# Attention beside a token-mixing MLP on one core: the first bias loaded in rows and turned over on TensorE, and a table of scheduling numbers by stretch

## The chip, the cores and the metric

One core of a Trainium2 chip runs the whole kernel. Its engines are TensorE (PE; its weight loads are shown apart as PEld), VectorE (DVE), ScalarE (ACT), GpSimd (POOL) and SyncE (SP, which issues most DMAs). The metric is device time in microseconds for one execution; the median of several executions is compared. Durations of single instructions come from one profiled execution.

## The reference

The input `x` has 2048 rows (tokens) of 512 columns, in bf16. It is layer-normalised; the result feeds an attention of 32 heads of 16 columns and, normalised once more, an MLP that mixes tokens: its matrices run over the 2048 tokens and a hidden width of 1376.

```
def _A_ref(x, wqkv, wo):
    qkv = split of (x @ wqkv) into q, k, v of 32 heads, 16 wide
    p = softmax(q @ k^T * 16 ** -0.5)
    return (p @ v, heads joined) @ wo

def _B_ref(x, w1, b1, w2, b2):
    h = _layernorm(x)
    u = gelu(einsum("bsd,sf->bdf", h, w1) + b1)
    y = einsum("bdf,fs->bds", u, w2) + b2
    return y transposed back to (b, s, d)

xn = _layernorm(A_x)
return A_x + _A_ref(xn, A_wqkv, A_wo) + _B_ref(xn, B_w1, B_b1, B_w2, B_b2)
```

`b1` has 1376 values, one for each hidden unit: ten rows of 128 and one of 96.

## The kernel before, in words

**Attention.** Queries are taken in 4 stretches of 512, heads in 8 groups of four: 32 blocks, worked in order. A block has 16 tiles of 128 keys, so there are 512 *groups* (block, key tile). The scores of a group are four matmuls (one for each of four heads, 32 rows of the array each, `score_mm`, L615) into four PSUM banks of 128 keys by 512 queries. A group goes one of two ways:

- On ACT ("A"): two `exp_tile` instructions (L638), each over two banks, write bf16 into `pT`. One set of four matmuls (`pv_mm`, L651) then multiplies by V into the block's PSUM bank (bank 6).
- On DVE ("D"): the exponential is made by arithmetic on the bits of a bf16. `dve_first` (L698) turns one bank into 16-bit integers, four times a group ("first step"); that is a plane. Two more planes are the first one plus a constant, made whole by one DVE instruction (`add_plane`, L711) or one POOL instruction (`add_plane_pool`, L718). Each of the three planes is multiplied by V in a set of its own, so a D group needs three sets of L651 where an A group needs one. `dve_first2` does the first step of two neighbouring banks in one instruction; the table before never allows it (`PAIR` is 0).

ACT rotates over banks 0 to 3. D scores use banks 4, 5 and 7, and so do all other products (the "chains": projections of q, k, v, both MLP layers, the output projection).

**Other work, in chains.** A `Chain` is a list of steps on named engines with a due position and a release position, counted in blocks. `chain_ut` makes one of the 11 hidden tiles of the MLP: 16 matmuls, then a DVE instruction (`u_evac`, L976) that adds the bias column `b1h[:, ft]`. `gelus` runs the gelu on ACT (L987). `chain_yo` makes the output rows. `chain_epi` ends a block: DVE copies the sums out of bank 6 (L1212), DMAs carry the denominators to DRAM and back (`den_scr`, `den_s`, `rec_scr`, `denb`), and POOL multiplies (L1249). `chain_qt` brings the next q rows into `QT` with eight DMAs on SP.

In most chains a 128-row product is issued as four matmuls of 32 output rows (`mm`, L541 to L555; L548 is a matmul, L547 a transpose). Such a quad is called a *unit*: at 512 columns it takes about as long as one full matmul.

**Order.** All instructions are put into a static order for each engine when the program is built. A dispatcher (`Sched` and the loop in the kernel function) keeps a clock for each engine with a cost for each instruction (917 ns for an exponential, 226 ns for a 512-column unit, 95 ns for a change between scores and other products, 450 ns for the issue of a DMA). At each moment it chooses what the engine does next: `pe_step` for PE (which also decides which group goes to ACT and which to DVE), `dve_step` for DVE, `misc_step` for POOL and SP. These choices depend on sixteen numbers:

```
TOL, JOIN, DEFER, P1_PRI, D_PEND, FAR, D_HUNGRY, PACE, N_SAME, PRESS, PL_PRI, D_LAST, SEED, PAIR, POOL_MIN, BURST
```

For example, `JOIN` is how long PE may wait for a DVE bank so that D scores join A scores in one visit; `POOL_MIN` is how much backlog DVE must have before POOL takes a plane; `PAIR` allows `dve_first2`; `SEED` varies some limits pseudo-randomly. The table `POLICY` holds rows of these numbers. Row n is read when the dispatcher's clock passes n times `SEG` = 10,000 ns, and the last row stays in force. Before, it has one row, so it holds throughout. Where PE has less than a given weight of units in the last 3.4 us of the dispatcher's clock, `pe_step` adds a filler: a unit of zeros accumulated into bank 6.

**The bias before.** At the start DVE clears `b1c_bf` (L442, 128 x 11), and two DMAs on SP fill it from the flat vector (L366), one value per partition, each value a 2-byte piece. Later, in `late_consts` (run once the work is a little past the first block), POOL turns it into fp32 in `b1h` (L460). `late_consts` also issues the loads of `wo_c` and `wo_pad`, and the first loads of `w1` and `w2` follow it on SP.

Of the kernel before, what the change touches and what calls it, by code (L numbers as in the profile page):

```python
# [10 lines left out]
BF16 = mybir.dt.bfloat16  # L11
# [8 lines left out]
F = 1376  # L20
NT = S // 128
NCT = D // 128
NFT = (F + 127) // 128
# [70 lines left out]


SEG = 10000.0
POLICY = [(130.0, 150.0, 300.0, -1, 0, 1300.0, 0.0, 0.05, 2, 3, 2, 7500.0, 0, 0.0, 1000.0, 2)]


SWITCH = 95.0  # L100
# [174 lines left out]
def bass_parallel_sum__softmax_full_mha__mixer_token_mlp__prompt_kernel(  # L275
# [18 lines left out]
    with ExitStack() as es:  # L294
        block = es.enter_context(nc.Block())

        def sb(name, shape, dt):
            return es.enter_context(nc.sbuf_tensor(name, shape, dt))
# [27 lines left out]
        w1blk = w1_flat[:, :].rearrange("p (s t j) -> p s t j", s=NW1, j=128)  # L326
        plx = sb("plx", [128, 2 * 2048], BF16)
        w2blk = sb("w2blk", [128, NW2, NFT, 128], BF16)
        b1c_bf = sb("b1c_bf", [128, NFT], BF16)
        b1h = sb("b1h", [128, NFT], F32)  # L330
        ident = sb("ident", [128, 128], BF16)
        stats = sb("stats", [128, NT, 6], F32)
# [6 lines left out]
        zw = sb("zw", [128, 128], BF16)  # L339
# [9 lines left out]
        sc = Sched(nc, es)  # L349
# [4 lines left out]
        PV_BANK = 6  # L354
        EX_BANK = 7

        def T_DVE(n, div=1.0):
            return dict(occ=(n / div + 64.0) / 0.96, lat=(n / div + 64.0) / 0.96 + 141.0)
# [3 lines left out]
        def dma(q, dst, src, reads, writes, name="", noncontig=False, out_dma=False, lat=2500.0, move=150.0):  # L362
            if noncontig:
                def fn(eng, dst=dst, src=src):
                    with nc.allow_non_contiguous_dma(reason="small strided transfer"):
                        return eng.dma_start(dst, src)  # L366
            else:
                def fn(eng, dst=dst, src=src):
                    return eng.dma_start(dst, src)
            op = sc.add(q, fn, reads=reads, writes=writes, name=name, dma=True, out_dma=out_dma, occ=450.0, lat=lat)  # L370

            dma_free[0] = max(dma_free[0], op.start + 1300.0) + move
            op.end = max(op.end, dma_free[0] + 700.0)
            heapq.heappush(sc.marks, op.end)
            return op
# [9 lines left out]
               reads=[("ident",)], writes=[("ident",)], occ=270, lat=400)  # L385
# [18 lines left out]
        for r in range(4):  # L404
            sc.add("pool", lambda e, r=r: e.memset(qmask[32 * r:32 * r + 16, 0:1], QSCALE),
                   reads=[("qmask",)], writes=[("qmask",)], occ=135, lat=145)
        sc.add("pool", lambda e: e.tensor_scalar(qmask[:, 1:2], qmask[:, 0:1], -1.0, QSCALE, ALU.mult, ALU.add),
               reads=[("qmask",)], writes=[("qmask",)], occ=190, lat=260)
# [14 lines left out]
        for t in range(NPRE):  # L423
            dma("sp" if t < 2 else "act", x_sb[:, t, :], x2[128 * t:128 * t + 128, :],
                reads=[("ident",)] if t == 2 else [], writes=[("x", t)], name="ld_x", lat=2150 + 150 * t)
# [4 lines left out]
               occ=1500)  # L430
# [8 lines left out]
        NFTF = F // 128  # L439
        MLAST = F - 128 * NFTF  # L440

        sc.add("dve", lambda e: e.memset(b1c_bf[:], 0.0), writes=[("b1c",), ("b1c2",)], occ=80)  # L442
        dma("sp", b1c_bf[:, 0:NFTF], B_b1[0:128 * NFTF].rearrange("(ft p) -> p ft", p=128),
            reads=[], writes=[("b1c",)], name="ld_b1a", noncontig=True, lat=13000)
        dma("sp", b1c_bf[0:MLAST, NFTF:NFTF + 1],
            B_b1[128 * NFTF:F].rearrange("(p o) -> p o", o=1), reads=[], writes=[("b1c2",)], name="ld_b1b",
            noncontig=True, lat=13000)

        def late_consts():
            sc.add("pool", lambda e: e.memset(wo_pad[:], 0.0),  # L450
                   writes=[("wo_pad", e_, r) for e_ in range(2) for r in range(4)], occ=900)
            sc.add("dve", lambda e: e.memset(gT[96:97, NFT - 1, :], 1.0), writes=[("gT1",)], occ=500)
            dma("sp", wo_c[:, :, :], A_wo.rearrange("(T q) n -> q T n", q=128), reads=[], writes=[("wo_c",)],
                name="ld_wo")
            for e_ in range(2):
                for r in range(4):
                    row = 3 * 128 + 32 * r + 16 * e_
                    dma("sp", wo_pad[32 * r:32 * r + 16, e_, :], A_wo[row:row + 16, :], reads=[],
                        writes=[("wo_pad", e_, r)], name="ld_wop")
            sc.add("pool", lambda e: e.tensor_copy(b1h[:], b1c_bf[:]), reads=[("b1c",), ("b1c2",)],  # L460
                   writes=[("b1h",)], occ=120, lat=230)


        def ln_stats0(t):
# [63 lines left out]
        ps_bf = ps.bitcast(BF16)  # L528

        def evac(eng, dst, src, reads, writes, n=512):  # L530
            if eng == "act":
                return sc.add("act", lambda e: e.activation(dst, src, ACTF.Identity), reads=reads, writes=writes,
                              occ=64 + n / 1.2, lat=242 + n / 1.2)
            return sc.add("dve", lambda e: e.tensor_copy(dst, src), reads=reads, writes=writes, **T_DVE(n))  # L534
# [3 lines left out]

        quad = [False]

        def mm(dst, lhsT, rhs, start, stop, reads, writes, n=512, m=128, turn=False):  # L541
            lat = 430.0 if n == 512 else 265.0
            occ = 226.0 if n == 512 else 56.0

            def form(e, a, b, pos):
                if turn:
                    return e.transpose(dst[a:b, :], lhsT[:, a:b], rhs, **pos)  # L547
                return e.matmul(dst[a:b, :], lhsT=lhsT[:, a:b], rhs=rhs, start=start, stop=stop, **pos)  # L548
            if not quad[0]:
                return sc.add("pe", lambda e: form(e, 0, m, {}), reads=reads, writes=writes, occ=occ, lat=lat, cfg="F")  # L550
            for a in range(0, m, 32):
                op = sc.add("pe", lambda e, a=a: form(e, a, min(a + 32, m), dict(tile_position=(0, a))),
                            reads=reads, writes=writes, name="q5" if n == 512 else "q1",
                            occ=(4.0 if a + 32 < m else occ - 12.0), lat=lat + 10.0, cfg="P")
            return op  # L555

# [3 lines left out]
        def kt_mm(T, c, ct, bk):  # L560
            return proj_mm(bank(bk), wqkv_sb[:, 1, ct, 128 * T:128 * T + 128],
                           xnT[:, c, ct, :], ct,
                           [("wqkv", 1, T)] + [("xnT", t) for t in range(4 * c, 4 * c + 4)], bk)

        def kt_evac(T, c, bk):
            return evac("dve", KT[:, T, 512 * c:512 * (c + 1)], bank(bk), reads=[("bank", bk)],
                        writes=[("KTt", T, t) for t in range(4 * c, 4 * c + 4)])
# [261 lines left out]
        pv_open = [True]  # L829
        TOL, JOIN, DEFER, P1_PRI, D_PEND, FAR, D_HUNGRY, PACE, N_SAME, PRESS, PL_PRI, D_LAST, SEED, PAIR, POOL_MIN, BURST = POLICY[0]  # L830
        kt_done = {0: 4}
# [50 lines left out]
        ex_queue = []  # L882
# [4 lines left out]
        def chain_kt(T, c, due, rel):  # L887
            bk = [EX_BANK]
            steps = [Step("pe", lambda ct=ct: kt_mm(T, c, ct, bk[0]), 226) for ct in range(NCT)]

            def fin():
                op = kt_evac(T, c, bk[0])
                kt_done[T] = kt_done.get(T, 0) + 1
                return op
            steps.append(Step("dve", fin, 610, frees=True))
            return Chain("kt%d.%d" % (T, c), steps, due, rel, bk=bk)

        def chain_vt(T, j, due, rel):
            bk = [EX_BANK]
# [768 lines left out]
        def pe_step(t):  # L1668

            t_s = None  # L1670
            if act_next():
                free_buf = [k for k in range(NPB if ln2_left[0] else NPB + NPX) if k not in buf_busy]
                if free_buf:
# [11 lines left out]
                    if t_s <= t + sw:  # L1685
# [3 lines left out]
                        p = act_cur[1].pop(0)  # L1689
# [34 lines left out]
            if tail["steps"] and part_done[0] == 4:  # L1724
                for z in tail["steps"]:
                    bk, fn, gate = z[0]
# [10 lines left out]
            if pv_open[0] and (not first or pv_block[0] == 0) and st_["pos"] < NBLK - 0.2 \  # L1737
                    and sc.ready(writes=[("bank", PV_BANK)], eng="pe") <= t:
                u = sum(w for a, w in pe_units(t))
                if u < (KEEP0 if t < T_KEEP0 else KEEP) and t + 226.0 + (SWITCH if sc.cfg == "S" else 0.0) <= lim:  # L1740
                    mm(bank(PV_BANK), zw[:], KT[:, 0, 0:512], first, first,
                       [("zw",)] + [("KTt", 0, q) for q in range(4)], [("bank", PV_BANK)])
                    n_zero[0] += 1
                    return True
            return False
# [11 lines left out]
        def pe_units(t):  # L1757
            z = []
            for o in reversed(sc.streams["pe"]):
                if o.start < t - 3413.0:  # L1760
                    break
                z.append((o.start, 1.0 if o.name == "" and o.occ > 200.0 else 0.0625 if o.name == "q1" else 0.25))
            return z
# [109 lines left out]
        while True:  # L1873
            guard += 1
            assert guard < 400000, "the dispatcher does not end"
            e = min(look, key=lambda q: look[q])
# [5 lines left out]
            while n_seg[0] * SEG <= t:  # L1882
                TOL, JOIN, DEFER, P1_PRI, D_PEND, FAR, D_HUNGRY, PACE, N_SAME, PRESS, PL_PRI, D_LAST, SEED, PAIR, POOL_MIN, BURST = POLICY[min(n_seg[0], len(POLICY) - 1)]
                n_seg[0] += 1
# [72 lines left out]
        if DEBUG_SCHED:  # L1957
            W = 25000.0
            n = int(max(sc.free.values()) / W) + 1
# [79 lines left out]
```

## Time and profile before

| | us |
|---|---|
| three runs | 671.85, 674.24, 669.07 |
| their median | 671.85 |
| the profiled execution | 668.16 |
| its span, first to last instruction | 666.4 |
| L638, all exponentials into `pT` (689) | 634.0 busy, 0.920 each |
| L698, all first steps (660) | 430.2 busy |
| L615, score matmuls (2048) | 279.3 busy |
| L460, the bias on POOL (1) | 0.25 |

Where instructions of a kind overlap, busy time divided by the count is the spacing of one; the mean duration (1122 ns for an exponential) also holds the part that overlaps. PE's busy time is modelled, since matmuls are pipelined, so a share near 100% doesn't by itself say that PE is the limit. The granted clock is the share of full TensorE speed. Names such as `x_sb`, `xnT` or `wqkv_sb` on lines L698, L711 and L718 are buffers whose first use is over and that serve as planes.

### The profile page before, as it was taken

The page shows a single profiled execution, that of the slowest core. Times are in us where ns is not written, and L with a number is a line of the kernel's source. Part 1 is how long each engine was busy: PE and PEld are TensorE (multiplying, and loading weights), DVE is VectorE, ACT ScalarE, POOL GpSimd, SP SyncE. Part 2 cuts the span into 40 slices and gives each one's busy share as a digit, 9 for nine tenths or more (in the row PEclk, how much of TensorE's full clock was granted, in tenths as well). Part 3 has the DMA queues.
Part 4 walks back from the last instruction along what each step waited for, and adds up shares of the span by engine and source line. Part 5 has one row for each costly group of instructions (what it writes and reads, how often), then busy time and mean ns, then how long its engine had stood idle before and what let it go on. Part 6 is the DMA issues. An engine that isn't in the chain of part 4 may idle for free.

```text
span 666.4 us, 21149 instructions
## 1 busy us (share of the span) xinstructions
PE 646.3 (97%) x9112; PEld 190.8 (29%) x9112; DVE 613.7 (92%) x1063; ACT 652.2 (98%) x713; POOL 394.3 (59%) x276
## 2 busy tenths in 40 slices
PE   8999999999999999999999999999999999999997
PEld 4543333322222222222222222222222222222222
DVE  7788999989999999998999999999999999999995
ACT  7899999999999999999999999999999999999996
POOL 5440476537465443668786675775577565556781
PEclk9899999999999999999999999999999999999999
DMA  8006100021222213210121222122021121312001
GB/s 222 4 17 144 35 15 21 25 57 34 63 55 55 52 30 70 41 30 19 34 53 46 60 59 56 35 50 66 18 53 25 53 55 42 98 38 54 28 23 49
DMA packets 78389, 33.01 MB, mean 50 GB/s; under 512 B 63004, under 2 KB 74204, under 8 KB 78296
## 3 DMA queue, kind: packets, MB, share of 16 engines
q1 hardware_dynamic: 77864, 31.27, 19.2%
q8 instruction: 71, 1.16, 0.7%
q10 hardware_dynamic: 432, 0.39, 0.2%
q14 instruction: 22, 0.18, 0.1%
HBM read 26.08 MB, written 2.61 MB: 43 GB/s over the span
## 4 chain that ended last, share of the span: by engine, by line
ACT 63%; PE 31%; DVE 3%; DMA 1%; issue 1%; SPq 0%; POOLq 0%; DVEq 0%
ACT pT L638 61%; PE ps L615 11%; PE ps L651 10%; PE ps L548 9%; ACT gT L987 1%; DVE stats L465 1%; PE ps L547 0%; DMA rec_scr<-den_s 0%; DMA x_sb<-in_A_x_dram 0%; DVE wqkv_sb L698 0%; DVE xnT L698 0%; DVE xn_sb L503 0%; DMA denb<-rec_scr 0%; ACT QT L576 0%; DVE w1blk L698 0%
## 5 line engine op out<-in xcount | busy, mean ns | idle before, releaser
L638 ACT ACTIVATE pT<-ps 128x1024 bf16<-128x1024 f32 x689 | 634.0, 1122 | 3.1 <-PE ps L615 2.5
L615 PE MATMUL ps<-QT,KT 32*128 32x512 bf16 x2048 | 279.3, 385 | 11.3 <-ACT pT L638 10.0
L615 PEld LDWEIGHTS ps<-QT,KT 32*128 32x128 bf16 x2048 | 71.2, 91 | 287.6 <-ACT pT L638 272.2
L698 DVE TENSOR_SCALAR x_sb<-ps 128x512 int16<-128x512 f32 x196 | 129.0, 682 | 8.8 <-PE ps L615 7.8
L651 PE MATMUL ps<-pT,V 128*32 128x512 bf16 x1378 | 133.4, 389 | 2.0 <-issue 1.4
L698 DVE TENSOR_SCALAR xn_sb<-ps 128x512 int16<-128x512 f32 x140 | 91.8, 683 | 8.5 <-PE ps L615 7.3
L698 DVE TENSOR_SCALAR xnT<-ps 128x512 int16<-128x512 f32 x100 | 65.3, 682 | 3.9 <-PE ps L615 3.3
L548 PE MATMUL ps<-h_sb,w1blk 128*32 128x512 bf16 x688 | 55.5, 383 | 0.0
L548 PE MATMUL ps<-gT,w2blk 128*32 128x512 bf16 (+1 forms) x704 | 55.2, 384 | 0.0
L651 PEld LDWEIGHTS ps<-pT,V 128*32 128x32 bf16 x1378 | 34.3, 94 | 64.0 <-issue 58.6
L698 DVE TENSOR_SCALAR plx<-ps 128x512 int16<-128x512 f32 x72 | 48.0, 685 | 3.9 <-PE ps L615 3.5
L698 DVE TENSOR_SCALAR wqkv_sb<-ps 128x512 int16<-128x512 f32 x68 | 44.5, 682 | 3.3 <-PE ps L615 3.1
L548 PE MATMUL ps<-xnT,wqkv_sb 128*32 128x512 bf16 (+2 forms) x680 | 41.1, 326 | 0.6 <-DVE xnT L534 0.5
L651 PE MATMUL ps<-x_sb,V 128*32 128x512 bf16 x364 | 35.2, 383 | 0.0
L698 DVE TENSOR_SCALAR w1blk<-ps 128x512 int16<-128x512 f32 x48 | 31.8, 683 | 2.4 <-PE ps L615 1.7
L718 POOL TENSOR_TENSOR x_sb<-xn_sb,shift_w 128x1024 int32<-128x1024 int32 x14 | 26.4, 1893 | 10.6 <-PE ps L615 4.8
L718 POOL TENSOR_TENSOR x_sb<-x_sb,shift_w 128x1024 int32<-128x1024 int32 x11 | 20.8, 1893 | 17.7 <-PE ps L548 5.5
L718 POOL TENSOR_TENSOR plx<-xn_sb,shift_w 128x1024 int32<-128x1024 int32 x8 | 15.1, 1893 | 26.6 <-DVE x_sb L711 20.6
L718 POOL TENSOR_TENSOR plx<-x_sb,shift_w 128x1024 int32<-128x1024 int32 x8 | 15.1, 1893 | 25.6 <-DVE x_sb L711 8.6
L718 POOL TENSOR_TENSOR xn_sb<-x_sb,shift_w 128x1024 int32<-128x1024 int32 x11 | 20.8, 1893 | 14.4 <-DVE wqkv_sb L711 7.4
L651 PE MATMUL ps<-xn_sb,V 128*32 128x512 bf16 x290 | 27.9, 382 | 0.1
L718 POOL TENSOR_TENSOR x_sb<-wqkv_sb,shift_w 128x1024 int32<-128x1024 int32 x8 | 15.1, 1893 | 19.5 <-DVE x_sb L711 8.8
(188 smaller groups left out, 874.5 us busy)
## 6 DMA issues: line engine op xcount, KB each, us to landing
denb<-rec_scr SPq DMA_DIRECT2D x124, 64.0 KB, 2.0
w1blk<-in_B_w_dram SPq DMA_DIRECT2D x10, 512.0 KB
w2blk<-in_B_w_dram SPq DMA_DIRECT2D x16, 320.0 KB, 6.2
xres<-in_A_x_dram SPq DMA_DIRECT2D x16, 128.0 KB, 2.1
QT<-qst SPq DMA_DIRECT2D x120, 16.0 KB, 1.8
out_dram<-osb SPq DMA_DIRECT2D x14, 128.0 KB, 1.7
wqkv_sb<-in_A_wqkv_dram SPq DMA_DIRECT2D x3, 384.0 KB, 7.5
x_sb<-in_A_x_dram SPq DMA_DIRECT2D x2, 512.0 KB, 6.4
```

Source lines behind the costliest of these rows:

```text
L465: return sc.add("dve", lambda e: e.bn_stats(stats[:, t, :], x_sb[:, t, :]), reads=[("x", t)], writes=[("stats", t)], occ=620, lat=725)
L548: return e.matmul(dst[a:b, :], lhsT=lhsT[:, a:b], rhs=rhs, start=start, stop=stop, **pos)
L615: return sc.add("pe", lambda e: e.matmul(bank(bk), lhsT=KT[32 * r:32 * r + 32, T, 128 * kt:128 * (kt + 1)], rhs=QT[32 * r:32 * r + 32, slo ...
L638: return sc.add("act", lambda e: e.activation(pT_buf(buf), ps[:, slot * 1024:(slot + 1) * 1024], ACTF.Exp, scale=EXP_SCALE), reads=[("bank ...
L651: return sc.add("pe", lambda e: e.matmul(bank(PV_BANK)[32 * r:32 * r + 32, :], lhsT=vt_[:, off:off + 32], rhs=rhs, start=start, stop=stop, ...
L698: return sc.add("dve", lambda e: e.tensor_scalar(plane_i[pb][:, 512 * r:512 * (r + 1)], bank(bk), BIAS, 0.0, ALU.add, ALU.max), reads=[("b ...
L718: return sc.add("pool", lambda e: e.tensor_tensor(plane_w[pb], plane_w[pb0], shift_w[:, j:j + 1].broadcast_to([128, 1024]), ALU.add), read ...
L987: op = sc.add("act", lambda e, m=m, f0=f0, f1=f1: e.activation(gT[0:m, f0:f1, :], gT[0:m, f0:f1, :], ACTF.Gelu_apprx_tanh), reads=[("gT", ...
```

## The change

1. `b1` is loaded late, in rows. The clearing of `b1c_bf` and its two DMAs at the start are gone. In `late_consts` POOL clears `b1r` (11 x 128), and two DMAs on SP load ten rows of 128 values and one of 96.
2. A new chain, `chain_b1`, turns `b1r` over on TensorE by transposes against the identity (11 columns, four of 32 output rows) into PSUM, and DVE copies the 128 x 11 result into `b1h`. POOL's copy is gone.
3. `POLICY` has 65 rows in place of one. Rows 0, 3, 15, 33 and 59 are the old row. In 25 rows `PAIR` isn't 0, `POOL_MIN` runs from 500 to 1800 and `SEED` is set in 33.
4. `mm` takes a name, and the fillers are named `qz`. The count of recent units weighs a unit of either name 0.25.

```diff
-POLICY = [(130.0, 150.0, 300.0, -1, 0, 1300.0, 0.0, 0.05, 2, 3, 2, 7500.0, 0, 0.0, 1000.0, 2)]
+POLICY = [
+    (130.0, 150.0, 300.0, -1, 0, 1300.0, 0.0, 0.05, 2, 3, 2, 7500.0, 0, 0.0, 1000.0, 2),
+    (85.0, 140.0, 500.0, -1, 0, 1300.0, 100.0, 0.1, 3, 4, 2, 8500.0, 0, 0.0, 1200.0, 0),
+    (175.0, 80.0, 500.0, -1, 0, 2000.0, 0.0, 0.2, 1, 5, 2, 8500.0, 18089, 0.0, 700.0, 2),
...
+    (200.0, 130.0, 200.0, -1, 1, 2000.0, 100.0, 0.05, 3, 2, 0.9, 6500.0, 0, 150.0, 1800.0, 2),
+]
...
-        b1c_bf = sb("b1c_bf", [128, NFT], BF16)
+        b1r = sb("b1r", [NFT, 128], BF16)
...
-        sc.add("dve", lambda e: e.memset(b1c_bf[:], 0.0), writes=[("b1c",), ("b1c2",)], occ=80)
-        dma("sp", b1c_bf[:, 0:NFTF], B_b1[0:128 * NFTF].rearrange("(ft p) -> p ft", p=128),
-            reads=[], writes=[("b1c",)], name="ld_b1a", noncontig=True, lat=13000)
-        dma("sp", b1c_bf[0:MLAST, NFTF:NFTF + 1],
-            B_b1[128 * NFTF:F].rearrange("(p o) -> p o", o=1), reads=[], writes=[("b1c2",)], name="ld_b1b",
-            noncontig=True, lat=13000)
...
-            sc.add("pool", lambda e: e.tensor_copy(b1h[:], b1c_bf[:]), reads=[("b1c",), ("b1c2",)],
-                   writes=[("b1h",)], occ=120, lat=230)
+            sc.add("pool", lambda e: e.memset(b1r[:], 0.0), writes=[("b1r",), ("b1r2",)], occ=120, lat=230)
+            dma("sp", b1r[0:NFT - 1, :], B_b1[0:128 * (NFT - 1)].rearrange("(ft p) -> ft p", p=128),
+                reads=[], writes=[("b1r",)], name="ld_b1a")
+            dma("sp", b1r[NFT - 1:NFT, 0:MLAST], B_b1[128 * (NFT - 1):F].rearrange("(o p) -> o p", o=1),
+                reads=[], writes=[("b1r2",)], name="ld_b1b")
+            ex_queue.append(chain_b1())
...
+        def chain_b1():
+            bk = [EX_BANK]
+
+            def turn():
+                return mm(ps_bf[:, bk[0] * 1024:bk[0] * 1024 + NFT], b1r[:], ident[0:NFT, 0:NFT], None, None,
+                          [("b1r",), ("b1r2",), ("ident",)], [("bank", bk[0])], 128, turn=True)
+
+            def fin():
+                return evac("dve", b1h[:], ps_bf[:, bk[0] * 1024:bk[0] * 1024 + NFT], [("bank", bk[0])], [("b1h",)], NFT)
+            return Chain("b1", [Step("pe", turn, 56), Step("dve", fin, 80, frees=True)], 1.6, 1.3, bk=bk)
...
                     mm(bank(PV_BANK), zw[:], KT[:, 0, 0:512], first, first,
-                       [("zw",)] + [("KTt", 0, q) for q in range(4)], [("bank", PV_BANK)])
+                       [("zw",)] + [("KTt", 0, q) for q in range(4)], [("bank", PV_BANK)], name="qz")
```

More of the change, by code (lines that the diff above doesn't have):

```diff
@@ L539, in bass_parallel_sum__softmax_full_mha__mixer_token_mlp__prompt_kernel, with mm @@
         quad = [False]
-        def mm(dst, lhsT, rhs, start, stop, reads, writes, n=512, m=128, turn=False):
+        def mm(dst, lhsT, rhs, start, stop, reads, writes, n=512, m=128, turn=False, name=None):
             lat = 430.0 if n == 512 else 265.0
@@ L552, in mm @@
                 op = sc.add("pe", lambda e, a=a: form(e, a, min(a + 32, m), dict(tile_position=(0, a))),
-                            reads=reads, writes=writes, name="q5" if n == 512 else "q1",
+                            reads=reads, writes=writes, name=name or ("q5" if n == 512 else "q1"),
                             occ=(4.0 if a + 32 < m else occ - 12.0), lat=lat + 10.0, cfg="P")
```

61 rows, old and new, of the table POLICY are left out of this document.

## The prediction

> **What bounds the kernel now.** I read the page's shares first, then the stretches, then the chain.
>
> ```profile
> PE 646.3 (97%) x9112; PEld 190.8 (29%) x9112; DVE 613.7 (92%) x1063; ACT 652.2 (98%) x713; POOL 394.3 (59%) x276
> ```
>
> That is the line of busy time, share and instructions. ACT is full, PE looks full, DVE has 8% left, POOL 41%. Busy time by stretch (columns: stretch, length, busy us of PE, PEld, DVE, ACT, POOL, granted clock, DMA):
>
> ```profile
> 75.00:375.00 300.00, 296.64 (x4052) 84.10 (x4044) 279.14 (x461) 299.76 (x324) 178.44 (x100) 1.00 0.18 42
> 375.00:525.00 150.00, 144.13 (x1816) 38.99 (x1812) 144.47 (x242) 149.88 (x165) 102.70 (x58) 1.00 0.19 46
> 525.00:625.00 100.00, 99.96 (x1279) 26.59 (x1275) 93.58 (x153) 99.94 (x110) 60.10 (x36) 1.00 0.23 58
> 625.00:650.00 25.00, 23.76 (x307) 6.43 (x299) 24.34 (x42) 25.00 (x28) 20.38 (x13) 1.00 0.06 17
> ```
>
> From 75 to 650 us ACT idles 0.42 of 575 us. No better order can remove waits of ACT there: only fewer exponentials on ACT shorten the kernel. The same stretches for VectorE's first step of its own groups (L698, four per group):
>
> ```profile
> 75.00:375.00 300.00, 206.24 (x316) 1.00 0.18 42
> 375.00:525.00 150.00, 114.83 (x178) 1.00 0.19 46
> 525.00:625.00 100.00, 69.50 (x105) 1.00 0.23 58
> 625.00:650.00 25.00, 21.15 (x34) 1.00 0.06 17
> ```
>
> VectorE takes 1.05 steps per us in the first and third row, 1.19 in the second, 1.36 in the fourth. So one fixed order uses VectorE unevenly, and that is the slack. Two pieces of the chain of waits show what PE can bear (columns: start, us, what):
>
> ```profile
> 127.89 186.24 ACT pT L638 x203
> ...
> 532.28 0.32 PE ps L615 x2
> 532.60 0.76 PE ps L651 x12
> 533.36 0.32 PE ps L615 x3
> 533.68 0.55 PE ps L651 x8
> ```
>
> For 186 us the chain is exponentials back to back. Near 532 us it is PE's: a visit to the scores is 0.32 us, two other units (quads of four matmuls) 0.55, three 0.76. A PE cycle is thus 0.87 or about 1.08 us, and ACT's is 0.921 (689 exponentials in 634.0 us, and five more, under another tile's name, in 5.5).
>
> **What a moved group is worth.** There are 512 groups. ACT has 694 exponentials, two per group, so 347 groups; VectorE has 660 first steps on the L698 rows, so 165. A group moved to VectorE takes 2 x 0.921 = 1.84 us off ACT. It gives VectorE four first steps (four in a row took 2.39 us in the chain, 0.60 each) and its share of two planes. The groups of lines that I added up hold 155 planes on VectorE (L711) and 175 on POOL (L718), so 0.94 per group on VectorE, at 0.60 (three in a row start 0.60 apart at 653.52, 654.12, 654.72). Together 2.4 + 0.56 = 2.96 us. On PE it adds two units and takes two exponential cycles away.
>
> **How many can move.** VectorE: from 75 to 650 us it idles 33.5 us. At the idle share of the second row (3.7%) it would idle 21.3. Each moved group takes 2.96 + 1.84 = 4.8 us of idleness, less 0.07 for the shorter stretch: 12.2 / 4.73 = 2.6 groups. POOL: it is busy 59.5% and 60.1% in rows one and three, 68.5% in row two. Brought up to that, it has 27.0 + 8.4 = 35.4 us, which is 18.7 planes at 1.89; these take 11.2 us off VectorE, or 2.4 groups. Sum 5.0 groups. PE: 842 units of value products (347 + 3 x 165), 539 of projections, MLP, output and fillers at 512 columns (688 + 704 + 432 + 240 + 92 records by four) and some 92 at 128 columns (1024 + 208 + 248 by sixteen) make 1473. (Of the 680 xnT,wqkv_sb records, 432 are the code's 27 chains of k and q, sixteen each.) At 2 + (0.921 - 0.870) / 0.22 = 2.23 units per cycle 694 cycles hold 1548, so 75 are free; a group takes 2 + 2 x 2.23 = 6.5: at most 11.6 groups. VectorE binds first. I take 5.0 groups, that is **-9.2 us**. The lower bound is 0: POOL's gaps are waits for VectorE's planes (38.0 us behind x_sb alone), and a new table need not fill them. The upper is VectorE at the fourth row's idle share (2.6%): 33.5 - 15 = 18.5, so 3.9 groups, and 2.4 from POOL: 6.3, or -11.6; 11.6 groups, -21.3, is PE's far end. I stand at the second row because it is the longest stretch that a fixed order has held.
>
> A rule speaks against the POOL term. The Trainium skill, "SBUF — State Buffer", section "SBUF: two separate sides", says that VectorE in a two-port mode and GpSimd take the port pair that they share as an exclusive lock, and the other blocks. The trace agrees as far as it shows: the last VectorE plane ahead of POOL's at 649.98 begins at 649.23, and POOL idled 0.96 us for it. By this rule alone the POOL term would go and the sum be 2.6 groups, -4.8 us.
>
> **The rest of the table.** Rows 1 and 2 act from 10 to 30 us, where ACT idles 2.07 and 0.55 us for PE, stuck behind the layernorm on VectorE. Bounds -2.6 and +2.6 (it may as well double); I take 0, as row 0, the prologue and the loads are unchanged. The paired first step (two banks in one instruction, allowed by 25 of the 65 rows) is not in the trace: between 0.68 us (the 128x1024 copy L534 into xnT) and 1.30 for two steps; I take 1.20, two back-to-back steps, so nothing.
>
> **The bias.** Removed: a 0.07 us VectorE clearing at 1.16 (PE's fillers begin behind it, but the first layernorm waits for x until 2.79), two issues on SP of 1.67 and 3.02 us from 9.30 to 14.03 (SP's next issue is at 41.57, so nobody is behind), their 1376 two-byte pieces, and a 0.25 us POOL copy at 47.46. If the pieces did delay the x tiles, their going gains up to the 2.07 us above; no layernorm wait after 9.3 us is put down to x. Added: a POOL clearing of about 0.20 (the 128x128 one of ident) and two row loads on SP at about 0.3 to 0.5 each (0.33 for a one-row b2 load, 0.47 for a wo_pad one) ahead of the first w1 loads (52.22); w1 is needed only before the first biased copy at 141.0. Behind them on SP stands the first block's den_scr store at 60.43: 0.8 us later, hidden while block 1's products run, otherwise 0.8 once. PE: four small transposes, 0.06 us inside other quads and up to 0.33 alone; VectorE: one 128x11 copy, about 0.24 (the 128x16 reciprocal), in a bank that a first step would have had. By VectorE's rate of exchange (1.84 us of span for 4.8 of idleness) that is 0.1 us. I take 0 for the bias; bounds -2.1 and +1.2. Filler matmuls get another name, but the planner counts them 0.25 as before: 0.
>
> **Sum.** Profiled execution: 668.16 us (span 666.4 and 1.76 around it) - 9.2 = 659.0. The runs' median, 671.85, stands 3.69 above that execution: **662.6 us**.
>
> **Rivals.** (a) The order changes, the split doesn't: 0 to 3.6 groups. For it: in 350-385 and 524-612 us the chain runs on PE, whose cycle of 0.87 or 1.08 averages ACT's pace, and the MLP's products must go somewhere. Against it: 61% of the span where the chain is L638's, in the second row with more first steps. At one group it is 670 us; all of it lies within 1%.
>
> (b) Slower: late hand-overs. Engines run a fixed order, so a block whose q rows or denominators land later than the planner thought stops PE, then ACT behind it. Place: SP's queue, where eight q rows took 4.97 to 6.18 us of issuing, against 450 ns each (3.6 us) in the planner's code; a POOL product waited 6.64 us for denb at the end. Against: ACT lost only 0.42 us in 575 to all such waits. At s us per block over 31 blocks, it eats the gain at s = 0.30 and is slower by 1% (6.7 us) from 0.51; at 0.75 it is 662.6 + 23 = 686 us.
>
> (c) PE's clock. From 10 to 20 us, with few matmuls, the granted clock was 0.84: 1.6 us of full-speed time lost. A table that leaves PE gaps pays that each time; ten times cancel the forecast and lose 6.8 us more: 679 us. Against: the clock is 1.00 in every stretch from 75 to 650, and PE is the fuller the more groups move. The Trainium skill, "TensorE: Matmul & The Clock Gate", section "What's actually happening", tells such a gate: half clock after an idle window of about 3.4 us. By that rule, too, the fillers' condition in the code, which the change leaves alone, stands against it.
>
> **Chances.** About 1% is what a measurement here can tell from none. Forecast (at least 3.7 groups) 0.66, its own range 656 to 665; (a) 0.24; (b) 0.07; (c) 0.03. So faster 0.66, same 0.24, slower 0.10. Low end: 6.3 groups, -11.6, and the start at -2.6 (the bias's gain is the same idle time) make 657.6, and one group on towards PE's end 656. High end: (a) at no group and the bias at its worst +1.2: 673. Outside lie (b), (c) and some forecasts past the low end, under 2 in 10.
>
> **What would show it.** Right: exponentials fall from 694 to about 684, first steps (paired ones counted twice) rise from 660 to about 680, ACT still idles under 1 us from 75 to 650, VectorE's idle share there falls from 5.8% to under 4.5%, POOL runs near 68%. Wrong: the count stays and so does the time (a); the count falls but ACT shows waits for L615 at block changes behind denb or QT (b); slices of clock under 9 past 30 us (c). If start or bias matter, ACT's idle time before 30 us moves by more than 1 us from 7.35.

## The result, and the profile after

| | before | changed |
|---|---|---|
| median of 13 runs each | 667.79 us | 663.25 us |
| ratio, 95% interval | | 0.9923 [0.9897, 0.9949] |
| profiled execution | 668.16 us | 662.49 us |
| its span | 666.4 us | 660.7 us |
| exponentials on ACT (two a group) | 694 | 686 |
| groups on VectorE | 165 | 169 |
| planes by POOL, by VectorE | 175, 155 | 191, 147 |

The change makes the kernel 0.77% faster, between 0.5% and 1.0%. The first three runs of before, which the prediction started from, had a median of 671.85 us; with ten more it is 667.79. That the forecast of 662.6 us lies 0.6 us from the measured 663.25 is luck: its base was 4.1 us too high, and its gain too large by about as much. The forecast was 9.2 us less; measured are 0.0077 x 668 = 5.1 us by the ratio, 4.5 between the medians, and 5.7 between the two profiled executions. The ratios here and below leave out three executions that were slow for their kernel: one of before (1042 us), one of bias_only (1317 us) and one of light_mlp (678.4 us). The granted clocks of the two profiled executions are equal in the first 30 us (0.94 each), so they compare well.

The changed kernel's line of engines, on its page:

```profile
PE 645.0 (98%) x9124; PEld 191.7 (29%) x9124; DVE 617.5 (93%) x1062; ACT 645.0 (98%) x705; POOL 423.8 (64%) x292
```

ACT has lost 7.2 us of work (652.2 to 645.0), which is 8 exponentials at 0.90 each, and POOL has gained 29.5. The busy time by stretch (stretch, length, busy us of PE, PEld, DVE, ACT, POOL, clock, DMA):

```profile
75.00:375.00 300.00, 299.10 (x4112) 85.36 (x4112) 283.96 (x464) 299.33 (x323) 197.32 (x112) 1.00 0.18 43
375.00:525.00 150.00, 145.54 (x1824) 39.28 (x1816) 145.24 (x241) 150.00 (x165) 113.44 (x64) 1.00 0.18 44
525.00:625.00 100.00, 99.84 (x1279) 26.98 (x1279) 94.12 (x156) 100.00 (x110) 65.19 (x39) 1.00 0.22 58
625.00:650.00 25.00, 24.28 (x310) 6.53 (x310) 24.20 (x42) 25.00 (x28) 16.11 (x9) 1.00 0.08 20
```

VectorE's idle time in these 575 us went from 33.5 to 27.5 us, POOL's busy share from 62.9% to 68.2%. The first steps in the same stretches, in the changed kernel (L761, one bank each):

```profile
75.00:375.00 300.00, 207.48 (x317) 1.00 0.18 43
375.00:525.00 150.00, 113.77 (x179) 1.00 0.18 44
525.00:625.00 100.00, 71.78 (x110) 1.00 0.22 58
625.00:650.00 25.00, 18.61 (x29) 1.00 0.08 20
```

To these come six paired steps in the first stretch and two in the second, which count double (the ninth pair starts at 650.2). That makes 329, 183 and 110 against 316, 178 and 105: from 75 to 625 us the gain is thin and spread, 3 to 5% more first steps in each stretch, not one place mended. The fourth stretch has fewer, 29 against 34, since the changed kernel is some 6 us nearer its end there.

Of the 7.2 us, 5.7 reach the end. ACT idles 15.7 us instead of 14.2: 0.3 less before 30 us, 0.7 more from 30 to 75 (0.62 of it one wait for PE at 48 us), 0.25 more from 75 to 650, and 0.8 more after the last exponential (8.23 us against 7.46).

### The profile page after: what moved, and what is told of

Read it like the earlier page. It is cut to its first block, busy times and chain, and to the rows that moved or that the text cites. A ratio compares the mean times of both kernels' runs of the same rounds, so it can differ in the third digit from the quotient of the medians.

```text
span 660.7 us, 21188 instructions
## 1 busy us (share of the span) xinstructions
PE 645.0 (98%) x9124; PEld 191.7 (29%) x9124; DVE 617.5 (93%) x1062; ACT 645.0 (98%) x705; POOL 423.8 (64%) x292
## 3 DMA queue, kind: packets, MB, share of 16 engines
q8 instruction: 72, 1.18, 0.8%
## 4 chain that ended last, share of the span: by engine, by line
ACT 60%; PE 33%; DVE 3%; DMA 1%; POOL 1%; issue 1%; POOLq 0%; SPq 0%; DVEq 0%
ACT pT L701 58%; PE ps L678 12%; PE ps L714 11%; PE ps L611 10%; ACT gT L1061 1%; PE ps L610 1%; ACT xn_sb L701 1%; POOL r L583 0%; DVE h_sb L587 0%; DVE w1blk L761 0%; DVE x_sb L769 0%; DVE xn_sb L774 0%; DMA x_sb<-in_A_x_dram 0%; DMA denb<-rec_scr 0%; DMA rec_scr<-den_s 0%
## 5 line engine op out<-in xcount | busy, mean ns | idle before, releaser
L761 DVE TENSOR_SCALAR x_sb<-ps 128x512 int16<-128x512 f32 x178 | 117.5, 683 | 8.1 <-PE ps L678 6.4
L761 DVE TENSOR_SCALAR xn_sb<-ps 128x512 int16<-128x512 f32 x120 | 78.3, 682 | 5.3 <-PE ps L678 4.7
L761 DVE TENSOR_SCALAR plx<-ps 128x512 int16<-128x512 f32 x110 | 72.5, 682 | 4.0 <-PE ps L678 3.5
L781 POOL TENSOR_TENSOR x_sb<-xn_sb,shift_w 128x1024 int32<-128x1024 int32 x18 | 33.9, 1890 | 41.1 <-PE ps L678 20.4
L761 DVE TENSOR_SCALAR xnT<-ps 128x512 int16<-128x512 f32 x84 | 55.6, 684 | 4.6 <-PE ps L678 3.7
L761 DVE TENSOR_SCALAR wqkv_sb<-ps 128x512 int16<-128x512 f32 x72 | 47.3, 680 | 2.4 <-PE ps L678 1.6
L761 DVE TENSOR_SCALAR w1blk<-ps 128x512 int16<-128x512 f32 x58 | 37.3, 681 | 1.7 <-PE ps L678 1.2
L781 POOL TENSOR_TENSOR x_sb<-plx,shift_w 128x1024 int32<-128x1024 int32 x15 | 28.2, 1891 | 15.1 <-DVE plx L761 6.0
L781 POOL TENSOR_TENSOR xn_sb<-x_sb,shift_w 128x1024 int32<-128x1024 int32 x15 | 28.4, 1893 | 9.1 <-DVE x_sb L769 3.8
L1323 POOL TENSOR_TENSOR oT<-OT,denb 128x512 bf16<-128x512 f32 x16 | 20.4, 1274 | 7.8 <-DVE wqkv_sb L774 7.8
L761 DVE TENSOR_SCALAR h_sb<-ps 128x512 int16<-128x512 f32 x36 | 23.5, 682 | 1.1 <-PE ps L678 1.0
```

Of the source, the lines that this page charges most:

```text
L761: return sc.add("dve", lambda e: e.tensor_scalar(plane_i[pb][:, 512 * r:512 * (r + 1)], bank(bk), BIAS, 0.0, ALU.add, ALU.max), reads=[("b ...
L781: return sc.add("pool", lambda e: e.tensor_tensor(plane_w[pb], plane_w[pb0], shift_w[:, j:j + 1].broadcast_to([128, 1024]), ALU.add), read ...
L1323: op = sc.add("pool", lambda e: e.tensor_tensor(dst, OT32[:, eb, :], denb[:, :], ALU.mult), reads=[("OT32", eb)] + [("denb", r) for r in r ...
```

## The experiments

My theory: the time is the number of exponentials on ACT at 0.921 us each, plus what is idle around them; the table acts by that number alone, through one particular order of the work. The rivals: the bias brings the gain; each row is a better policy for its stretch; the gain lies in the first or last stretches alone.

**Which part of the change it is.** Old table with the new bias, new table with the old bias, and the changed kernel with its rows in reversed order ("..." stands for what is left out):

```diff
 # bias_only: the changed kernel
-POLICY = [ ...65 rows... ]
+POLICY = [(130.0, 150.0, 300.0, -1, 0, 1300.0, 0.0, 0.05, 2, 3, 2, 7500.0, 0, 0.0, 1000.0, 2)]
...
 # table_only: the kernel before
-POLICY = [(130.0, 150.0, 300.0, -1, 0, 1300.0, 0.0, 0.05, 2, 3, 2, 7500.0, 0, 0.0, 1000.0, 2)]
+POLICY = [ ...65 rows... ]
...
 # rows_reversed: the changed kernel
-POLICY = [row 0, row 1, ... row 64]
+POLICY = [row 64, row 63, ... row 0]
```

> The bias in rows, with the old table of one row; 165 groups on VectorE, so 694 exponentials, as before. My theory (the gain is the count of exponentials, 0.921 us each) expects the time of before within 1.3 us: ratio 0.998 to 1.002, and the 10 to 20 us stretch still with some 2 us of ACT idle. The rival, that the bias brings the gain (2-byte pieces gone from the start), expects about -4.5 us, ratio 0.993.

> The bias as before, with the 65 rows. Only the small bias steps differ from the changed kernel, but the choices fall out otherwise: 162 groups on VectorE, 700 exponentials. By the count, 6 x 0.921 = 5.5 us slower than before: ratio 1.008. The rival, that each row is better for what is done in its stretch, expects the changed kernel's gain nearly whole: ratio 0.993.

> The changed kernel with its 65 rows in reversed order; the order made from it has 160 groups on VectorE, 704 exponentials. By the count, 10 x 0.921 = 9.2 us slower than before: ratio 1.014. The rival, that the rows are better numbers wherever they stand, expects no more than before: ratio 1.000 or under.

| kernel | exponentials | expected by the count | measured (ratio, interval) |
|---|---|---|---|
| bias_only | 694 | 0 | +0.7 us (1.001 [0.998, 1.004]) |
| table_only | 700 | +5.5 us | +11.0 us (1.0164 [1.013, 1.020]) |
| rows_reversed | 704 | +9.2 us | +9.2 us (1.0137 [1.008, 1.019]) |
| the changed kernel | 686 | -7.4 us | -5.1 us (0.9923 [0.990, 0.995]) |

(Measured us are the ratio less one times 668.) The bias is worth nothing that can be measured. The table alone makes the kernel *slower*. PE's instructions in the two traces are the same, kind by kind, until 54 us, about where the changed kernel turns its bias (55.7 us); from there the choices fall otherwise, and the same rows then lead to 162 groups on VectorE, not 169. So in these two other orders the rows are no better numbers in themselves; they fit one order. Reversed, they cost what the count says, within an interval of 5.6 to 12.7 us. The rival on the rows falls; only table_only misses the count, by 5.5 us.

**What table_only lost besides.** Three lines of its windows show the place (columns as above):

```profile
580.00:600.00 20.00, 20.00 (x260) 5.41 (x256) 19.07 (x33) 20.00 (x23) 9.85 (x6) 1.00 0.22 58
600.00:620.00 20.00, 18.38 (x202) 4.32 (x202) 14.73 (x24) 17.08 (x19) 11.63 (x9) 0.87 0.24 56
620.00:640.00 20.00, 20.00 (x249) 5.25 (x246) 18.46 (x31) 19.20 (x21) 6.45 (x5) 0.96 0.11 30
```

ACT loses 3.7 us there, and the granted clock falls. Its timeline tells why (start, us, engine, line, what, idle time before it and its releaser; lines between are left out):

```profile
606.02 5.62 SPq L435 DMA_DIRECT2D QT<-qst  x8
611.69 0.58 SPq L435 DMA_DIRECT2D xres<-in_A_x_dram  x1
613.98 0.69 DVE L1163 TENSOR_TENSOR h_sb<-ps,xres 128x512 f32<-128x512 f32 x1 [2.19 <-DMA xres<-in_A_x_dram]
614.73 0.60 PE L681 MATMUL ps<-QT,KT 32*128 32x512 bf16 x1 [1.09 <-DVE h_sb L1163]
617.38 1.02 ACT L704 ACTIVATE pT<-ps 128x1024 bf16<-128x1024 f32 x1 [2.35 <-PE ps L681]
618.90 1.02 ACT L704 ACTIVATE pT<-ps 128x1024 bf16<-128x1024 f32 x1 [0.50 <-PE ps L681]
620.42 1.02 ACT L704 ACTIVATE pT<-ps 128x1024 bf16<-128x1024 f32 x1 [0.50 <-PE ps L681]
```

SP spends 5.62 us on issuing eight q rows, and the load of xres (rows of the input, which are added to the output) stands behind them. VectorE waits 2.19 us for xres and holds a bank, PE waits for VectorE, ACT for PE. After PE's pause its granted clock is 0.50 from 616 to 621 us (a score matmul's record is 0.60 us, not 0.39), and for some cycles one cycle takes 1.52 us, where ACT would need 0.92. So this late hand-over costs twice: the wait, and then the slow PE. That is two of the prediction's rivals in a row. Another 2.8 us of table_only's extra idle time stand behind ACT's last exponential (10.2 us instead of 7.5) and were not followed up. To test the stop, the xres load goes ahead of the q rows on SP, in the two places where q rows stand directly before it:

```diff
+        for op in [o for o in spq if o.name == "ld_xres"]:
+            i = j = spq.index(op)
+            while j > 0 and spq[j - 1].name == "q_rows":
+                j -= 1
...
+            spq.insert(j, spq.pop(i))
...
         sc.plan()
```

> The kernel of table_only with SP's order changed in two places: the load of xres goes ahead of the eight q rows that stood directly before it (planned at 553 and at 604 us); nothing else moves. If the 2.35 us stop of ACT near 617 us, and the half-speed PE behind it, come from xres queued behind eight q rows on SP (5.62 us of issuing), both go: ACT's idle time from 500 to 640 falls from 3.7 to under 1 us and the time from 680.1 to about 676.5 (ratio to before 1.011). The rival, that VectorE or PE is late there for itself, expects the stop where it was.

The stop is gone:

```profile
500.00:640.00 140.00, 136.87 (x1714) 36.59 (x1718) 132.06 (x217) 140.00 (x153) 78.34 (x47) 1.00 0.19 48
```

ACT is busy all of the 140 us (table_only: 136.28) and the clock stays at 1.00, so the cause of the stop is shown. The time is less clear: four runs, 675.62, 675.63, 681.35 and 682.41 us, and the ratio of 1.0152 [1.009, 1.021] can't be told from table_only's. The profiled one is the 681.35; it lost 2.2 us before 30 us and 1.2 from 30 to 75 against table_only's profile, nearly all of the 3.7 that it won. The mean granted clocks on record sort the runs: xres_first's two short ones have 0.998, its two long ones 0.986; table_only has 679.04 and 679.31 us at 0.996, 680.89 and 681.14 at 0.990. Between the short pairs lie 3.6 us, which is the forecast; but this pairing was made after the result, and rests on two runs each. More on that start below.

**Half of the table, and nine new rows.** If the count is all, half a table should give about half the gain, and other rows with the same count the same gain.

```diff
 # first_48_rows
-POLICY = [row 0, ... row 64]
+POLICY = [row 0, ... row 47, the row of before]
 # nine_rows_new: rows 14, 19, 47, 53, 54, 56, 58, 63, 64 changed, for example row 53
-    (90.0, 120.0, 200.0, -1, 1, 1300.0, 0.0, 0.05, 1, 5, 2, 9500.0, 73998, 0.0, 500.0, 2),
+    (170.0, 90.0, 400.0, -1, 0, 2000.0, 0.0, 0.1, 2, 5, 2, 9500.0, 0, 150.0, 1100.0, 2),
...
```

> The changed kernel with its first 48 rows, and the old row from 480 us on: the order is the changed kernel's up to there; 167 groups on VectorE, 690 exponentials. By the count 4 x 0.921 = 3.7 us under before, ratio 0.9945, about half of the way. The rival, that the gain lies in the first or the last stretches alone, expects either the changed kernel's time (0.992) or that of before (1.000).

> The changed kernel with nine rows (14, 19, 47, 53, 54, 56, 58, 63, 64) drawn anew; the order keeps 169 groups, 686 exponentials, and has a shorter tail by the planner's clock. By the count the same time as the changed kernel, within 1.5 us either way: ratio to before 0.990 to 0.995. If the numbers of the rows held more than their draw, nine new rows would lose some of the gain.

| kernel | exponentials | expected by the count | measured (ratio, interval) |
|---|---|---|---|
| first_48_rows | 690 | -3.7 us | -4.1 us (0.9938 [0.991, 0.997]) |
| nine_rows_new | 686 | -7.4 us | -5.4 us (0.9919 [0.989, 0.995]) |

Both fit. The interval of first_48_rows also touches that of the changed kernel, so "half" is shown by the count and only likely by the time: that the gain lies in the last stretches alone is out, that it lies in the first alone is not ruled out by the time. The changed kernel's 110 first steps against 105 from 525 to 625 us speak against it. nine_rows_new is at the changed kernel's level, but it is a weak test of other rows: row 14 differs in one number, rows 19 and 58 in two, and VectorE's instructions are the same, kind by kind, as the changed kernel's up to 480 us.

**Which engine bounds the count.** The prediction worked out a limit for VectorE and one for PE apart. Each was taken away in turn, under the old one-row table.

```diff
 # half_first_step: the first step works on 256 of a bank's 512 columns (the planner's cost too)
...
-plane_i[pb][:, 512 * r:512 * (r + 1)], bank(bk)
+plane_i[pb][:, 512 * r:512 * r + 256], bank(bk)[:, 0:256]
...
 # light_mlp: two of sixteen token tiles, two of eleven hidden tiles
-steps = [Step("pe", lambda st=st: ut_mm(st), 226) for st in range(NT)]
+steps = [Step("pe", lambda st=st: ut_mm(st), 226) for st in (0, NT - 1)]
...
-for ft in range(NFT):
+for ft in (0, NFT - 1):
 # light_both: both
```

> Old table of one row, bias in rows. VectorE's first step does the left 256 of 512 columns of a bank only (the other columns of the planes keep what was there; one clearing of plx is added on POOL), so VectorE has some 175 us less to do and is no limit. My prediction's counts: with VectorE out of the way PE allows up to 11.6 more groups than 165; the order made has 173, so 678 exponentials, 16 x 0.921 = 14.7 us under the bias_only kernel: span near 651. If instead VectorE alone set the limit, as my sum took it, 175 us would have moved 175 / 4.8 = 36 groups and the span would be near 600.

> Old table, bias in rows. The MLP's products leave out 14 of 16 token tiles in the first layer and 9 of 11 hidden tiles in the second (154 + 144 units of 0.22 us, 65 us of PE less). With PE out of the way VectorE is what is left: my prediction gave it 5.0 groups. The order made has 169, 686 exponentials, 7.4 us under bias_only: span near 658. If PE alone set the limit, 298 units would be worth 298 / 6.5 = 46 groups, span near 580.

> Both at once: half the first step and the short MLP products. The order made has 185 groups, 654 exponentials: 40 x 0.921 = 36.8 us under bias_only, span near 628 to 630. That the two together move 20 groups, and alone 8 and 4, is what two nearly equal limits would show. The rival, that something else (the three PSUM banks, ACT's pace) caps VectorE's groups, expects the order to run with PE and VectorE both well under 90% busy and no more than 12 groups' worth of time, span above 642.

| kernel | groups on VectorE | span by the count | span of the profiled run | ACT idle in it | all runs (ratio to before) |
|---|---|---|---|---|---|
| bias_only | 165 | | 664.9 | 12.6 | 1.001 [0.998, 1.004] |
| half_first_step | 173 | 651 | 659.2 | 19.8 | 0.985 [0.971, 0.9985], two runs |
| light_mlp | 169 | 658 | 672.2 | 25.4 | 1.004 [0.999, 1.010] |
| light_both | 185 | 629 | 638.6 | 21.5 | 0.959 [0.951, 0.968], two runs |

The counts are what the dispatcher makes of its own costs, so they test the prediction's sum, not the chip: +8 with VectorE out of the way (PE's limit; the sum had 11.6), +4 with PE out of the way (VectorE's limit; the sum had 5.0), +20 with both. The two limits are close together, and neither engine's work alone sets the count. light_both ran with VectorE 80% and PE 93% busy and 20 more groups, so ACT's pace doesn't cap them. The three banks are not ruled out: a first step on half a bank lets go of the bank sooner, and a chain with 2 MLP products instead of 16 or 11 holds its bank for less time, so both edits relieve the banks as well.

The profiled times missed by 8 to 14 us; the step from count to time failed, in all three mostly through ACT's idle time. In half_first_step 3.3 us of it lie before 30 us, where the granted clock is 0.83 (in bias_only 1.00, with the same order there), and 3.3 behind the last exponential. Its other execution had a span of 653.1 us, 2 us from the count. In light_mlp it is table_only's chain of events again, in the timeline (lines between are left out):

```profile
396.45 5.80 SPq L371 DMA_DIRECT2D QT<-qst  x8
402.29 0.58 SPq L371 DMA_DIRECT2D xres<-in_A_x_dram  x1
404.72 0.69 DVE L1093 TENSOR_TENSOR osb<-ps,xres 128x512 bf16<-128x512 f32 x1 [2.00 <-DMA xres<-in_A_x_dram]
407.52 1.02 ACT L637 ACTIVATE pT<-ps 128x1024 bf16<-128x1024 f32 x1 [1.54 <-PE ps L614]
```

ACT lost 8.5 us between 350 and 600, with the clock at 0.97 over that stretch. Not each of its stops was followed back to SP, and not each pause of PE slows its clock: around ACT's waits near 456 and 532 us the clock is 1.00. In the changed kernel such stops don't occur: ACT's idle time is 0.67 us in the 575. Why some orders have them and others don't was not tried.

**The tail.** In the changed kernel the tail is 0.8 us longer. POOL's last product with denb started at 652.81, one microsecond after denb had landed; the wait is put down to a plane on VectorE, because the planner lets POOL wait for VectorE's last two-port instruction:

```profile
652.04 0.69 DVE L774 TENSOR_SCALAR wqkv_sb<-xn_sb 128x2048 int16<-128x2048 int16 x1
652.81 1.27 POOL L1323 TENSOR_TENSOR oT<-OT,denb 128x512 bf16<-128x512 f32 x1 [5.89 <-DVE wqkv_sb L774]
```

I took that one wait away.

```diff
 def mul():
...
+    if b == NBLK - 2:
+        sc.two = None        # POOL doesn't wait for VectorE's last plane
     op = sc.add("pool", lambda e: e.tensor_tensor(dst, OT32[:, eb, :], denb[:, :], ALU.mult),
...
```

> The changed kernel's order with one wait less: POOL's last product with denb (block 30) no longer waits for VectorE's last plane in a two-port mode, which the planner made it do. If that wait is what kept it from 651.8 (denb landed) to 652.8, it now starts within 0.2 us of denb's landing and the span falls by 0.7 to 0.9 us (ratio to before about 0.991). The rival, that the two engines' shared port holds it as long, expects the product to start where it did, and no gain over the changed kernel.

The timeline of that kernel at its end, which runs 1.6 us later than the changed kernel's profile because of its start:

```profile
653.59 1.30 POOL L1325 TENSOR_TENSOR oT<-OT,denb 128x512 bf16<-128x512 f32 x1 [5.04 <-DMA denb<-rec_scr]
...
653.06 0.69 DVE L774 TENSOR_SCALAR xnT<-xn_sb 128x2048 int16<-128x2048 int16 x1
653.67 1.77 DVE L774 TENSOR_SCALAR wqkv_sb<-xn_sb 128x2048 int16<-128x2048 int16 x1
```

The product now starts when denb lands. But VectorE's next plane, 0.08 us behind it, takes 1.77 us instead of 0.69: it ends 0.55 us after POOL's product, so nearly all of its work comes behind it. From the store of the block's reciprocals to the end it is 14.15 us, against 14.08 in the changed kernel. The rival is right on the gain, though not on the start: the wait changed sides. The runs (662.95 us, ratio 0.991 [0.987, 0.994]) can't be told from the changed kernel's.

Nor was this wait what made the tail longer. Counted from that store, the kernel before takes 14.51 us to its end, more than the changed kernel's 14.08. What differs is ACT: its last exponential ends 5.8 us after the store instead of 7.1. So at the very end the time doesn't go with ACT, and some 0.8 us of what ACT saved don't reach the end.

## Why the prediction was right, and where its sizes were off

**The mechanism** was right. The time goes with the exponentials on ACT; ACT idles 0.67 us from 75 to 650 (forecast: under 1); the counts are 686 and 676 first steps, paired ones counted twice (forecast 684 and 680); POOL is 68.2% busy (forecast 68). One sign missed: VectorE's idle share from 75 to 650 us was to fall under 4.5%, and is 4.8%.

**The size.** The forecast was 5.0 groups and -9.2 us; it is 4 groups, and -5.7 us between the profiled executions. Two terms were mis-sized. The first is VectorE's: "at the idle share of the second row (3.7%) it would idle 21.3", worth 2.6 groups. It idles 27.5 us, 4.8%: 6.0 us of 12.2 were found, 1.3 groups. POOL's term held: 16 planes more against 18.7, 2.0 groups or so. These make 3.3; the rest lies outside that stretch, where VectorE idles 3.6 us less, 0.8 groups by the same exchange. The second is that all of 1.84 us per group reaches the end: 1.5 us came back as idle time of ACT, at 48 us (table_only has that wait too, bias_only hasn't) and in the tail, where the prediction had no term.

**The chances.** The likeliest case, over 1% faster, didn't come: four groups were enough for its condition, but not, after what came back, for its bound. What came lies in the case "within 1%", at its edge.

**The base.** Three runs of before were 4 us above what thirteen gave. That 662.6 us came so near is luck: this error and the missing part of the gain cancelled. From 667.79 the same sum gives 658.6, still within the forecast's own range of 656 to 665. A spread of 5 us among three should have been read as the bound of the base, not only of the result.

**The rule against the POOL term.** The Trainium skill's exclusive lock ("SBUF — State Buffer", "SBUF: two separate sides") fits what the tail showed, 1.08 us more for a plane where the two instructions meet. It didn't cancel the POOL term: 16 more planes fit into POOL's gaps, with the planner's waits keeping the two apart.

**The rivals.** (a), order without a different split, is refuted by the count. (b), late hand-overs on SP's queue, and (c), PE's clock, didn't happen in the changed kernel. Both happened in table_only and light_mlp, and at the stops shown they came together; the prediction kept them apart and priced (c) at 1.6 us an event, without the late hand-over ahead of it.

**The bias.** Taken as 0, measured +0.7 us [-1.1, +2.5]. Its parts: POOL's clearing 0.19 us (0.20 forecast), the row loads' issues 0.22 and 0.40 (0.3 to 0.5), VectorE's copy 0.16 (0.24). A paired first step lasts 1.22 us, but a part of that overlaps with the next instruction: where VectorE doesn't wait, the next one starts 1.13 to 1.18 us after it (seven of the nine), against the 1.20 taken for two single steps. So "nothing" was right to within 0.1 us a pair.

## What to carry to other kernels

When three engines are full, a new order is worth only what it moves off the fullest one: count the instructions that move, and price them at their spacing. A table of numbers that fits one order is part of that order: change a small step ahead of it, and the numbers have to be found anew, or they can cost more than they gave. And a load queued behind a burst of small DMA issues is late by the burst's issue time; look for it where the waits name a DMA that is itself short.

## What the runs showed of the hardware that was not expected

**The start differs from run to run by some 3 us, with PE's clock.** PE stops for 1.4 to 1.6 us near 15.6 us, marked "issue", in the profiles that I looked at closely (before, the changed kernel, first_48_rows, table_only). Afterwards its granted clock stays at 1.00, or is low for a few microseconds, or stays low to 30 us and past it. The length of the stop doesn't decide: in the changed kernel and in first_48_rows it is 1.5 us, and from 19 to 22 us the clock is then 0.61 in the one and 1.00 in the other. Mean granted clock and ACT's busy us of the first 30, each from one profiled execution:

| granted clock, 0 to 30 us | ACT busy, 0 to 30 us | kernels |
|---|---|---|
| 1.00 | 24.0, 24.3 | bias_only, first_48_rows |
| 0.94 | 21.6 to 23.0 | before, changed, table_only, tail_no_wait, light_mlp, light_both, nine_rows_new |
| 0.82 to 0.83 | 20.4 to 20.8 | rows_reversed, half_first_step, xres_first |

The order isn't the cause: in these 30 us bias_only, light_mlp and half_first_step have the same instructions, kind by kind, on PE, VectorE, ACT and POOL, and ACT is busy for 24.0, 22.4 and 20.6 us of them. Two lines, bias_only's and then that of half_first_step:

```profile
0.00:30.00 30.00, 25.35 (x614) 13.51 (x614) 24.51 (x69) 23.98 (x33) 16.91 (x53) 1.00 0.43 125
```

```profile
0.00:30.00 30.00, 24.85 (x488) 12.85 (x492) 21.23 (x57) 20.64 (x29) 14.65 (x48) 0.83 0.42 125
```

PE is shown as busy for about the same 25 us but does 488 matmuls instead of 614, and ACT does 3.3 us less. This may account for a good part of the spread among runs of one kernel: of the 21 runs of before beside first_48_rows, the six with a mean clock of 1.000 over the span took 666.0 to 667.1 us, the three with 0.986 to 0.989 took 671.8 to 673.9. That their clock was lost in the start is shown for the profiled executions alone. What stops PE at 15.6 us, and what decides on the clock after it, was not tried and stays open. The Trainium skill, "TensorE: Matmul & The Clock Gate", section "What's actually happening", says that the window by which the gate judges runs freely, so that the moment differs from run to run; that would fit, and no run here shows the window itself.
